# Sliding-window attention in front of two MLPs on one core: scores as plain float32 products in place of three split passes

## The chip, the cores and the metric

The kernel runs on one core of one Trainium2 chip. The metric is device time in microseconds of one execution; lower is better. Before the change three executions took 939.21, 941.5 and 942.63 us (median 941.5). The profiled execution took 941.04 us.

## What is computed

Three blocks in a row, all in float32. Attention has 4 batches, 8 heads, 576 positions and head size 64, with a causal window of 128 positions and a linear bias by distance. A gated MLP (512 to 1536) and a second MLP (512 to 2048) follow, over 2304 tokens. The reference, cut to what matters:

```python
scores = scale * np.matmul(q, k.transpose(0, 1, 3, 2))      # scale = 1/8
scores = np.where((rel >= 0) & (rel < 128), scores + bias, -1e9)
attn = softmax(scores)
x = np.matmul(attn, v)                                      # to 2304 x 512
g = x @ w_gate; x = (silu(g) * (x @ w_val)) @ w_out         # 512 -> 1536 -> 512
g = x @ w_in;   return silu(g) @ w_out2                     # 512 -> 2048 -> 512
```

## The kernel before, in words

Tokens are taken in 18 tiles of 128. Tiles 0 to 5 are part 0, 6 to 11 part 1, 12 to 17 part 2; the MLPs run part by part on 768 tokens. Each tile has two halves (`hf`) of four heads, so there are 36 halves.

The MLP products want nearly float32 accuracy. Their operands are split in two: a high part rounded to `float32r` and a low part that is the rest. Each product is three passes, high by high, high by low and low by high (`passes`, lines 803 to 807; `out1`, 963 to 965; `out2`, 993 to 995). Splitting costs a copy and a subtraction on the side engines for every operand. The scores use the same form:

- `prepare` (lines 389 to 425) turns k and q of one half with the identity on TensorE (`k_turn`, line 401; `q_turn`, line 409). From PSUM it writes the high part of k (`copy_op`, line 304 on ScalarE or 305 on VectorE) and of q (`q_hi`, line 412, ScalarE, with the factor -1/8). Then VectorE subtracts to get the low parts (`k_lo`, line 404; `q_lo`, line 415).
- `score` (lines 429 to 457) makes the products. For each half there are two head pairs `p`, three passes `(x, y)` and two heads `e` of a pair. The two heads lie in rows 0 to 63 and 64 to 127 of the array and write two different banks. That is 12 products of 128 weight columns by 256 moving columns (current and previous tile of keys). In tiles 0 and 9, the first of their part of the sequence, there are 128 moving columns.
- `attend` masks on VectorE (line 476, a `copy_predicated` that reads the scores), adds the bias and takes the row minimum (483), exponentiates on ScalarE (489), normalizes on GpSimd (509) and turns the weights with TensorE (526). `weigh` multiplies by v (line 563). v and the turned weights are plain float32 there, and two heads write PSUM partitions 0 to 63 and 64 to 127.

The order on each engine is not written by hand. `Plan.add` records every operation with an engine, an estimated cost in ns, a due time, the keys it reads and writes, and the PSUM bank it takes or gives back. `Plan.issue` then plays a list schedule with those costs and issues each engine's instructions in the order it found. At run time each engine keeps that order and waits on semaphores. Part 0's attention has due times over the first 45 us or so (`ramp`) and the MLP begins beside it. The attention of parts 1 and 2 is spread between MLP products. A wrong cost moves the order, not the time an instruction takes. The cost of the scores stands in line 456:

```python
plan.add("pe", 6 * 118 * len(halves) + 290, due, products, reads, list(take), take=take)
```

Of the kernel before, what the change touches and what calls it, by code (L numbers as in the profile page):

```python
# [9 lines left out]
F32 = mybir.dt.float32  # L10
F32R = mybir.dt.float32r
# [5 lines left out]
AF = mybir.ActivationFunctionType  # L17
ALU = mybir.AluOpType
PSUM = bass.MemoryType.PSUM

P = 128
# [180 lines left out]
def attention_moe_moe2_kernel(  # L202
# [34 lines left out]
    nc = tc.nc  # L237
    B, H, S, D = q.shape
# [13 lines left out]
    big = ctx.enter_context(tc.tile_pool(name="big", bufs=1))  # L252
# [3 lines left out]
    def ring(n, shape, dtype, name):  # L256
        return [big.tile(shape, dtype, name=f"{name}{i}") for i in range(n)]
# [2 lines left out]
    XOP = big.tile([P, 7, 2, 2, N], F32R, name="XOP")  # L260
    XST = big.tile([P, PT, KC, P], F32, name="XST")
    ACC = big.tile([P, PT, KC, P], F32, name="ACC")
    KR = big.tile([P, 2, H // 2, 2, P], F32R, name="KR")
    ident = big.tile([P, P], F32, name="ident")
    alibi = big.tile([P, H, P], BF16, name="alibi")
    bigt = big.tile([P, 2, P], F32, name="bigt")
# [11 lines left out]
    KLD_R = ring(2, [P, H, D], F32, "kld")  # L278
    QLD_R = ring(2, [P, H, D], F32, "qld")
    VLD_R = ring(3, [P, H, D], F32, "vld")  # L280
    QT_R = ring(2, [P, 2, 2, P], F32R, "qt")
    C_R = ring(2, [P, 4, P], F32, "c")
    ST_R = ring(2, [P, 3, 4], F32, "st")
    U_R = ring(3, [P, 4, P], F32, "u")
# [12 lines left out]
    plan = Plan(BANKS, {"mm": 6, "att": 6, "T": 1, "S": 4, "C": 2, "O": 1, "B": 4})  # L297

    def cost(kind, n):
        a, b = COST[kind]  # L300
        return a + b * n

    def copy_op(n, due, out, src, reads, writes, give=None, psum=True):
        act = lambda: nc.scalar.activation(out(), src(), AF.Copy)  # L304
        dve = lambda: nc.vector.tensor_copy(out(), src())
        plan.add(
            "act", cost("act_ps" if psum else "act", n), due, act, reads, writes, give=give,
            other=[("dve", cost("dve", n), dve, not psum, 500.0)],
        )
# [46 lines left out]
    def first(i):  # L356
        return (i * P) % S == 0
# [27 lines left out]
    def loaded(i, nm, hf):  # L385
        slot = i % (3 if nm == "v" else 2)
        return [(nm, slot, hf, r) for r in range(2)]

    def prepare(i, hf, due):
        kn, qn = KLD_R[i % 2], QLD_R[i % 2]  # L390
        kr = KR[:, :, 2 * hf:2 * hf + 2, i % 2, :]
        bk, bq = Bank("T"), Bank("T")
        pk = lambda: bk.tile.rearrange("p (a b) -> p a b", b=P)
        pq = lambda: bq.tile.rearrange("p (a b) -> p a b", b=P)
        slot = (2 * i + hf) % len(QT_R)
        qt = QT_R[slot]

        def k_turn():
            for j in range(2):
                h = 4 * hf + 2 * j  # L400
                nc.tensor.transpose(pk()[:, j, :], kn[:, h:h + 2].rearrange("p h d -> p (h d)"), ident)

        def k_lo():
            nc.vector.tensor_tensor(kr[:, 1], pk()[:, 0:2], kr[:, 0].bitcast(F32), ALU.subtract)

        def q_turn():
            for j in range(2):
                h = 4 * hf + 2 * j
                nc.tensor.transpose(pq()[:, j, :], qn[:, h:h + 2].rearrange("p h d -> p (h d)"), ident)

        def q_hi():
            nc.scalar.activation(qt[:, 0], pq()[:, 0:2], AF.Copy, scale=-0.125)

        def q_lo():
            nc.vector.scalar_tensor_tensor(
                qt[:, 1], pq()[:, 0:2], -0.125, qt[:, 0].bitcast(F32), ALU.mult, ALU.subtract
            )

        kk, qk = ("KR", i % 2, hf), ("qt", slot)
        plan.add("pe", 2 * 109, due, k_turn, loaded(i, "k", hf) + ["ident"], [bk], take=bk)  # L420
        copy_op(256, due, lambda: kr[:, 0], lambda: pk()[:, 0:2], [bk], [kk])
        plan.add("dve", cost("dve", 256), due, k_lo, [bk, kk], [kk], give=bk)
        plan.add("pe", 2 * 109, due, q_turn, loaded(i, "q", hf) + ["ident"], [bq], take=bq)
        plan.add("act", cost("act_ps", 256), due, q_hi, [bq], [qk])
        plan.add("dve", cost("dve", 256), due, q_lo, [bq], [qk], give=bq)

    def score(i, halves, due):

        s = i % 2
        banks = {hf: (Bank("S"), Bank("S")) for hf in halves}

        def products():
            for hf in halves:
                qt = QT_R[(2 * i + hf) % len(QT_R)]  # L440
                for p in range(2):
                    for x, y in ((0, 0), (0, 1), (1, 0)):
                        for e in range(2):
                            rows = slice(64 * e, 64 * e + 64)
                            view = banks[hf][e].tile.rearrange("p (a b c) -> p a b c", a=2, b=2)
                            rhs, dst = KR[rows, y, 2 * hf + p], view[:, p]
                            if first(i):
                                rhs, dst = rhs[:, s], dst[:, 0]
                            nc.tensor.matmul(  # L449
                                dst, qt[rows, x, p, :], rhs, start=(x == 0 and y == 0), stop=(x == 1)  # L450
                            )

        reads = [("qt", (2 * i + hf) % len(QT_R)) for hf in halves]
        reads += [("KR", t, hf) for t in ((s,) if first(i) else (s, 1 - s)) for hf in halves]
        take = tuple(b for hf in halves for b in banks[hf])
        plan.add("pe", 6 * 118 * len(halves) + 290, due, products, reads, list(take), take=take)
        return banks

    def attend(i, hf, dues, banks):
# [563 lines left out]
    def attention_part(part, at):  # L1023
        for i in range(part * PT, part * PT + PT):
            load(i, "k", at(i) - 14820.0)
            load(i, "q", at(i) - 20070.0)
            load(i, "v", at(i) - 7670.0)
            for halves in [(0,), (1,)] if i < EARLY else [(0, 1)]:
                t0 = at(i + 0.5 * halves[0])
                for hf in halves:  # L1030
                    prepare(i, hf, t0 - 8000.0)
                banks = score(i, halves, t0)
                for hf in halves:
                    attend(i, hf, [at(i + p / NP) for p in (2 * hf, 2 * hf + 1)], banks[hf])
                weigh(i, halves, at(i + 0.5 * halves[-1] + 1 / NP))
# [136 lines left out]
```

## Time and profile before

| What | Value |
|---|---|
| profiled execution | 941.04 us, span 939.3 us |
| median of three runs | 941.5 us |
| TensorE matmul (PE) busy | 916.3 us, 98% |
| VectorE (DVE) busy | 669.3 us, 71% |
| ScalarE (ACT) busy | 503.4 us, 54% |
| GpSimd (POOL) busy | 352.3 us, 38% |

Busy time of PE includes the time in which a matmul drains, so 98% is not 98% of its peak. A line number names the line of the kernel that issued an instruction; 304, 305, 313 and 314 are lines of helpers (a copy on ScalarE or VectorE, a sum on VectorE or GpSimd). PEld is TensorE's weight load, which overlaps PE. One product in the program can show as one or two matmul records in the trace.

### The profile page before, as it was taken

How to read it: one execution, taken by the hardware profiler on the slowest of the kernel's cores; microseconds unless marked ns; L12 is line 12 of the kernel's file. 1: busy time of each engine (PE TensorE's matmuls, PEld its weight loads, DVE VectorE, ACT ScalarE, POOL GpSimd, SP SyncE). 2: the span in 40 equal slices, each digit the busy share in tenths (PEclk: the TensorE clock that was granted, in tenths of full speed). 3: DMA queues.
4: the chain of work that ended last, by engine and by line, in shares of the span. 5: the costliest groups of instructions: out<-in, count | busy, mean ns of one | idle time of the engine just before them, and what ended most of it. 6: DMA issues, size and time to landing. Idle time of an engine off the chain costs nothing.

```text
span 939.3 us, 16799 instructions
## 1 busy us (share of the span) xinstructions
PE 916.3 (98%) x5626; PEld 845.3 (90%) x5626; DVE 669.3 (71%) x1536; ACT 503.4 (54%) x1276; POOL 352.3 (38%) x416
## 2 busy tenths in 40 slices
PE   7999999998999999999999999999999999999998
PEld 5799899998888888999999888888899999988887
DVE  8988779879889888637574847567735555855655
ACT  6887567757867675654343564354343322553331
POOL 3865568776657578772122512111100000300000
PEclk9999999999999999999999999999999999999999
DMA  9987997895897987986666655445576666655422
GB/s 226 280 250 244 289 316 242 275 334 176 278 304 261 301 297 266 335 294 204 189 201 188 174 186 162 169 153 172 187 238 211 205 212 210 201 185 179 157 91 90
DMA packets 156855, 209.79 MB, mean 223 GB/s; under 512 B 65760, under 2 KB 86496, under 8 KB 156768
## 3 DMA queue, kind: packets, MB, share of 16 engines
q1 hardware_dynamic: 156768, 208.71, 69.3%
q8 instruction: 45, 0.74, 0.3%
q14 instruction: 42, 0.34, 0.1%
HBM read 149.42 MB, written 59.24 MB: 222 GB/s over the span
## 4 chain that ended last, share of the span: by engine, by line
PE 76%; DVE 10%; DMA 5%; ACT 4%; POOL 3%; issue 3%; SPq 0%; DVEq 0%; POOLq 0%; ACTq 0%
PE bank L805 13%; PE bank L806 12%; PE bank L807 12%; PE bank L993 6%; PE bank L995 6%; PE bank L994 6%; PE bank L963 4%; PE bank L965 4%; PE bank L964 4%; PE bank L563 3%; PE bank L449 3%; DVE word L707 2%; PE bank L526 1%; DMA raw<-in_moe_w_out_dram 1%; DMA raw<-in_moe_w_in_dram 1%
## 5 line engine op out<-in xcount | busy, mean ns | idle before, releaser
L805 PE MATMUL bank<-XOP,wu 128*128 128x384 f32 (+1 forms) x868 | 297.2, 342 | 8.4 <-ACT tmp L304 2.6
L806 PE MATMUL bank<-XOP,wu 128*128 128x384 f32 (+1 forms) x868 | 289.6, 334 | 3.7 <-POOL XOP L314 3.0
L807 PE MATMUL bank<-XOP,wu 128*128 128x384 f32 (+1 forms) x868 | 289.4, 333 | 0.0
L805 PEld LDWEIGHTS bank<-XOP,wu 128*128 128x128 f32 x868 | 163.6, 188 | 17.8 <-ACT tmp L304 5.2
L806 PEld LDWEIGHTS bank<-XOP,wu 128*128 128x128 f32 x868 | 163.8, 189 | 6.0 <-POOL XOP L314 3.5
L807 PEld LDWEIGHTS bank<-XOP,wu 128*128 128x128 f32 x868 | 163.6, 189 | 0.2
L304 ACT ACTIVATE tmp<-bank 128x384 f32<-128x384 f32 x156 | 73.2, 489 | 108.6 <-PE bank L807 71.8
L314 POOL TENSOR_TENSOR h<-tmp,h 128x384 fp32r<-128x384 f32 x48 | 51.4, 1079 | 187.0 <-ACT h L304 185.7
L993 PE MATMUL bank<-wo,h 128*128 128x512 f32 x290 | 115.8, 399 | 0.3 <-DVE bank L649 0.3
L995 PE MATMUL bank<-wo,h 128*128 128x512 f32 x290 | 114.0, 393 | 0.0
L994 PE MATMUL bank<-wo,h 128*128 128x512 f32 x290 | 113.9, 393 | 0.0
L1005 DVE TENSOR_TENSOR ACC<-bank,ACC 128x512 f32<-128x512 f32 (+1 forms) x127 | 85.3, 681 | 26.9 <-PE bank L995 26.7
L845 DVE TENSOR_TENSOR bank<-bank,tmp 128x384 f32<-128x384 f32 x108 | 60.5, 561 | 57.8 <-PE bank L807 43.4
L963 PE MATMUL bank<-h,wo 128*128 128x384 f32 (+1 forms) x296 | 99.3, 335 | 0.1
L965 PE MATMUL bank<-h,wo 128*128 128x384 f32 (+1 forms) x296 | 98.3, 332 | 0.0
L964 PE MATMUL bank<-h,wo 128*128 128x384 f32 (+1 forms) x296 | 98.0, 331 | 0.0
L977 DVE TENSOR_TENSOR ACC<-bank,ACC 128x384 f32<-128x384 f32 x120 | 65.5, 553 | 28.1 <-PE bank L965 27.8
L922 DVE SCALAR_TENSOR_TENSOR tmp<-tmp,bank 128x384 f32<-128x384 f32 (+1 forms) x101 | 53.9, 542 | 44.3 <-ACT tmp L912 31.4
L304 ACT ACTIVATE h<-tmp 128x384 fp32r<-128x384 f32 x81 | 42.0, 522 | 70.6 <-PE bank L994 45.7
L912 ACT ACTIVATE tmp<-bank 128x384 f32<-128x384 f32 (+1 forms) x131 | 62.1, 483 | 32.0 <-PE bank L807 18.1
L509 POOL TENSOR_TENSOR c<-c,st 128x512 f32<-128x512 f32 x36 | 39.6, 1101 | 98.4 <-DVE st L506 83.2
L489 ACT ACTIVATE c<-c,st 128x128 f32<-128x128 f32 x144 | 56.3, 394 | 25.6 <-DVE st L483 25.5
(96 smaller groups left out, 1642.5 us busy)
## 6 DMA issues: line engine op xcount, KB each, us to landing
wo<-kept_o SPq DMA_DIRECT2D x56, 512.0 KB, 4.0
wu<-kept_i SPq DMA_DIRECT2D x112, 256.0 KB, 3.3
wu<-kept_g SPq DMA_DIRECT2D x72, 256.0 KB, 3.6
wu<-kept_v SPq DMA_DIRECT2D x72, 256.0 KB, 4.0
raw<-in_moe_w_out_dram SPq DMA_DIRECT2D x28, 512.0 KB, 4.8
kept_o<-wo SPq DMA_DIRECT2D x28, 512.0 KB, 4.2
kept_i<-wu SPq DMA_DIRECT2D x56, 256.0 KB, 4.3
kept_g<-wu SPq DMA_DIRECT2D x42, 256.0 KB, 4.8
```

The source lines that it names most:

```text
L304: act = lambda: nc.scalar.activation(out(), src(), AF.Copy)
L805: nc.tensor.matmul(ps, wh, xh, start=start, stop=False, skip_group_check=True)
L806: nc.tensor.matmul(ps, wh, xl, start=False, stop=False, skip_group_check=True)
L807: nc.tensor.matmul(ps, wl, xh, start=False, stop=stop, skip_group_check=True)
L963: nc.tensor.matmul(ps[:, 0:n], wh, h[:, 0], start=(i == 0), stop=False)
L964: nc.tensor.matmul(ps[:, 0:n], wh, h[:, 1], start=False, stop=False)
L965: nc.tensor.matmul(ps[:, 0:n], wl, h[:, 0], start=False, stop=(i == 1))
L977: plan.add("dve", cost("dve", n), due, lambda: nc.vector.tensor_tensor(acc, pv(), acc, ALU.add), [b], keys, give=b)
L993: nc.tensor.matmul(ps, hh, wh, start=(i == 0), stop=False)
L994: nc.tensor.matmul(ps, hh, wl, start=False, stop=False)
L995: nc.tensor.matmul(ps, hl, wh, start=False, stop=(i == 1))
L1005: plan.add("dve", cost("dve", n), due, lambda: nc.vector.tensor_tensor(acc, pv(), acc, ALU.add), [b], keys, give=b)
```

## The change

q and k are no longer split. `KR` and the `qt` buffers lose their axis of two and become plain float32. `prepare` keeps the two turns, one copy of k and one scaled copy of q, and loses both subtractions. Each bank is given back by the copy. `score` makes one plain float32 product per head, four per half, and its planned cost becomes 2 * 236 per half.

```diff
-    KR = big.tile([P, 2, H // 2, 2, P], F32R, name="KR")
+    KR = big.tile([P, H // 2, 2, P], F32, name="KR")
-    QT_R = ring(2, [P, 2, 2, P], F32R, "qt")
+    QT_R = ring(2, [P, 2, P], F32, "qt")
...
-        def k_lo():
-            nc.vector.tensor_tensor(kr[:, 1], pk()[:, 0:2], kr[:, 0].bitcast(F32), ALU.subtract)
...
-        def q_hi():
-            nc.scalar.activation(qt[:, 0], pq()[:, 0:2], AF.Copy, scale=-0.125)
-
-        def q_lo():
-            nc.vector.scalar_tensor_tensor(
-                qt[:, 1], pq()[:, 0:2], -0.125, qt[:, 0].bitcast(F32), ALU.mult, ALU.subtract
-            )
+        def q_copy():
+            nc.scalar.activation(qt, pq()[:, 0:2], AF.Copy, scale=-0.125)
...
-        copy_op(256, due, lambda: kr[:, 0], lambda: pk()[:, 0:2], [bk], [kk])
-        plan.add("dve", cost("dve", 256), due, k_lo, [bk, kk], [kk], give=bk)
+        copy_op(256, due, lambda: kr, lambda: pk()[:, 0:2], [bk], [kk], give=bk)
...
-        plan.add("act", cost("act_ps", 256), due, q_hi, [bq], [qk])
-        plan.add("dve", cost("dve", 256), due, q_lo, [bq], [qk], give=bq)
+        plan.add("act", cost("act_ps", 256), due, q_copy, [bq], [qk], give=bq)
...
-                    for x, y in ((0, 0), (0, 1), (1, 0)):
-                        for e in range(2):
-                            rows = slice(64 * e, 64 * e + 64)
...
-                            nc.tensor.matmul(
-                                dst, qt[rows, x, p, :], rhs, start=(x == 0 and y == 0), stop=(x == 1)
-                            )
+                    for e in range(2):
+                        rows = slice(64 * e, 64 * e + 64)
...
+                        nc.tensor.matmul(dst, qt[rows, p, :], rhs, start=True, stop=True)
...
-        plan.add("pe", 6 * 118 * len(halves) + 290, due, products, reads, list(take), take=take)
+        plan.add("pe", 2 * 236 * len(halves) + 290, due, products, reads, list(take), take=take)
```

The line numbers of the changed kernel are smaller: line 449 becomes 438, 409 becomes 406, 476 becomes 463, 483 becomes 470, 526 becomes 513, 563 becomes 550, 707 becomes 694.

On PE, one half of an early tile before (names are `out<-moving,weights`; `bank` is a PSUM bank, `KR` and `qt` hold k and q, `u` and `l` the turned attention weights, `vld` is v):

```order
L449 MATMUL bank_140<-KR,qt_125 128x256
L449 MATMUL bank_138<-KR,qt_125 128x256
L449 MATMUL bank_140<-KR,qt_125 128x256
L449 MATMUL bank_138<-KR,qt_125 128x256
L449 MATMUL bank_140<-KR,qt_125 128x256
L449 MATMUL bank_138<-KR,qt_125 128x256
L449 MATMUL bank_140<-KR,qt_125 128x256
L449 MATMUL bank_138<-KR,qt_125 128x256
L449 MATMUL bank_140<-KR,qt_125 128x256
L449 MATMUL bank_138<-KR,qt_125 128x256
L449 MATMUL bank_140<-KR,qt_125 128x256
L449 MATMUL bank_138<-KR,qt_125 128x256
```

and with the change, with the products by v that stand behind it:

```order
L438 MATMUL bank_140<-KR,qt_125 128x256
L438 MATMUL bank_141<-KR,qt_125 128x256
L438 MATMUL bank_140<-KR,qt_125 128x256
L438 MATMUL bank_141<-KR,qt_125 128x256
L550 MATMUL bank_135<-u_130,vld_121 64x128 x2
L550 MATMUL bank_135<-l_134,vld_122 64x128 x2
L550 MATMUL bank_135<-u_130,vld_121 64x128 x2
L550 MATMUL bank_135<-l_134,vld_122 64x128 x2
```

Twelve products of a half have become four; in all, PE's list shrinks from 5036 to 4748 rows, by 288 = 36 x 8.

On DVE, the first instructions behind the constants, before (`m_up` and `bigt` are masks and fill values, `c` and `st` scores and their row sums):

```order
L415 SCALAR_TENSOR_TENSOR qt_124<-bank_135,qt_124 128x256
L415 SCALAR_TENSOR_TENSOR qt_125<-bank_136,qt_125 128x256
L404 TENSOR_TENSOR KR<-bank_137,KR 128x2x128
L404 TENSOR_TENSOR KR<-bank_138,KR 128x2x128
L476 COPY_PREDICATED bank_139<-m_up,bigt 128x2x128
L483 ISA c_126,st_128<-bank_139,alibi 128x128
```

and with the change, the same place and, apart, the first copy of k that VectorE takes from ScalarE:

```order
L463 COPY_PREDICATED bank_139<-m_up,bigt 128x2x128
L470 ISA c_126,st_128<-bank_139,alibi 128x128
...
L492 TENSOR_SCALAR st_128<-st_128 128x4
L493 RECIPROCAL st_128<-st_128 128x4
L305 COPY KR<-bank_138 128x2x128
L492 TENSOR_SCALAR st_129<-st_129 128x4
```

The four subtractions ahead of the first mask are gone. Over the program VectorE loses 36 of each kind and takes 3 of the 36 copies of k; ScalarE keeps the other 33.

## Rows read from the trace of the kernel before

**Rows 1.** The page, busy time, share and instructions of each engine.
```profile
PE 916.3 (98%) x5626; PEld 845.3 (90%) x5626; DVE 669.3 (71%) x1536; ACT 503.4 (54%) x1276; POOL 352.3 (38%) x416
```
**Rows 2.** Busy time by stretch: stretch, length, engines' busy us (instructions), granted clock, DMA.
```profile
0.00:46.00 46.00, 38.57 (x335) 30.41 (x336) 39.05 (x166) 34.76 (x119) 25.30 (x34) 1.00 0.97 256
...
60.00:400.00 340.00, 330.37 (x2079) 304.09 (x2079) 286.78 (x635) 236.50 (x606) 231.86 (x276) 0.99 0.85 279
400.00:660.00 260.00, 258.73 (x1607) 239.86 (x1607) 163.28 (x386) 119.36 (x303) 70.38 (x81) 1.00 0.60 188
660.00:939.00 279.00, 274.69 (x1482) 258.43 (x1478) 168.57 (x312) 100.98 (x212) 15.62 (x15) 1.00 0.55 182
```
**Rows 3.** The chain of waits, first 50 us: start, length, what.
```profile
22.55 0.33 DVE KR L404
...
23.87 0.34 DVE KR L404
...
27.36 0.89 PE bank L449 x12
...
41.04 0.33 DVE KR L404
...
42.82 0.32 DVE qt L415
...
45.45 0.42 DVE KR L404
```
**Rows 4.** Groups of instructions on DVE, whole run: count, busy us, mean ns.
```profile
L404 DVE TENSOR_TENSOR KR<-bank,KR 128x256 fp32r<-128x256 f32 x36 | 15.0, 417 | 7.3 <-ACT KR L304 7.1
L415 DVE SCALAR_TENSOR_TENSOR qt<-bank,qt 128x256 fp32r<-128x256 f32 x36 | 14.9, 415 | 3.5 <-ACT qt L412 3.4
```
**Rows 5.** The same groups, 0 to 46 us.
```profile
L404 DVE TENSOR_TENSOR KR<-bank,KR 128x256 fp32r<-128x256 f32 x11 | 4.5, 412 | 1.1 <-ACT KR L304 1.1
L415 DVE SCALAR_TENSOR_TENSOR qt<-bank,qt 128x256 fp32r<-128x256 f32 x10 | 4.0, 411 | 0.6 <-ACT qt L412 0.5
```
**Rows 6.** Timeline of PE, score products: start, busy us, line, records.
```profile
135.10 1.65 PE L449 MATMUL bank<-KR,qt 64*128 64x256 f32 x24
136.68 0.45 PE L805 MATMUL bank<-XOP,wu 128*128 128x384 f32 x1
```
```profile
241.84 1.56 PE L449 MATMUL bank<-KR,qt 64*128 64x128 f32 x24
243.33 0.50 PE L993 MATMUL bank<-wo,h 128*128 128x512 f32 x1
```
**Rows 7.** The same, 323.6 to 324.3 us; and line 449's records, min/median/max ns.
```profile
323.39 1.09 PE L449 MATMUL bank<-KR,qt 64*128 64x256 f32 x16
```
```profile
L449 PE MATMUL bank<-KR,qt x432: 270/273/579, 6.3 to 623.4; 64*128 64x256 f32 x128, 64*128 64x128 f32 x16
```
**Rows 8.** Timeline of PE, products by v in plain float32.
```profile
115.36 0.39 PE L563 MATMUL bank<-u,vld 128*64 128x128 f32 x4
...
116.45 0.39 PE L563 MATMUL bank<-l,vld 128*64 128x128 f32 x4
```
**Rows 9.** Line 449 by stretch: PE and PEld busy us (records).
```profile
46.00:660.00 614.00, 22.62 (x324) 19.70 (x324) 1.00 0.74 240
```
**Rows 10.** Timeline of PE, score products near the start.
```profile
8.41 1.55 PE L449 MATMUL bank<-KR,qt 64*128 64x128 f32 x12
...
11.05 1.90 PE L449 MATMUL bank<-KR,qt 64*128 64x256 f32 x12
```
**Rows 11.** Who waited for whom on PE, 60 to 400 us: total us, times, longest.
```profile
PE bank L805 <- DVE tmp L860: 2.4, 3, 1.1
...
PE bank L805 <- DVE tmp L305: 1.7, 2, 1.0
```
**Rows 12.** The same on DVE, whole run.
```profile
DVE bank L476 <- PE bank L449: 5.2, 8, 1.6
```

More of the change, by code (lines that the diff above doesn't have):

```diff
@@ L390, in prepare @@
         kn, qn = KLD_R[i % 2], QLD_R[i % 2]
-        kr = KR[:, :, 2 * hf:2 * hf + 2, i % 2, :]
+        kr = KR[:, 2 * hf:2 * hf + 2, i % 2, :]
         bk, bq = Bank("T"), Bank("T")
@@ L441, in products @@
                 for p in range(2):
-                    for x, y in ((0, 0), (0, 1), (1, 0)):
-                        for e in range(2):
-                            rows = slice(64 * e, 64 * e + 64)
[L445 to L448, printed above, removed]
-                            nc.tensor.matmul(
-                                dst, qt[rows, x, p, :], rhs, start=(x == 0 and y == 0), stop=(x == 1)
-                            )
+                    for e in range(2):
+                        rows = slice(64 * e, 64 * e + 64)
+                        view = banks[hf][e].tile.rearrange("p (a b c) -> p a b c", a=2, b=2)
+                        rhs, dst = KR[rows, 2 * hf + p], view[:, p]
+                        if first(i):
+                            rhs, dst = rhs[:, s], dst[:, 0]
+                        nc.tensor.matmul(dst, qt[rows, p, :], rhs, start=True, stop=True)
         reads = [("qt", (2 * i + hf) % len(QT_R)) for hf in halves]
```

## The prediction

> **What bounds the kernel now.** I read the page's busy time first: PE is busy 98% of the span, DVE 71% [rows 1]. Then I split the span by stretch. From 60 us on PE is busy 330 of 340, 259 of 260 and 275 of 279 us [rows 2]. There, TensorE time added or removed is span added or removed. The first 46 us are different: PE is busy 38.6 us and DVE 39.1 [rows 2], and the chain of waits runs through DVE and ACT as well as PE. Five pieces of that chain are the subtractions that the change deletes [rows 3]. So the change has two separate accounts: PE time after 46 us, and the start.
>
> **VectorE: removed work.** 36 subtractions for k and 36 for q, 15.0 + 14.9 = 29.9 us [rows 4]. Nothing is added but three copies of k from ScalarE, which I price like a subtraction of the same size, 0.42 us each [rows 4].
>
> - *Start.* The pieces on the chain are 0.33 + 0.34 + 0.33 + 0.32 + 0.42 = 1.74 us [rows 3]. Two groups of score products also lie on it, the one at 27.36 us [rows 3] and another like it at 32 us; each grows by 0.17 (below). Net -1.74 + 0.34 = -1.4 us. Bounds: 0, if a chain right behind takes over (ACT has 34.8 us of work in these 46 [rows 2]); and 4.5 + 4.0 = 8.5 us if DVE alone sets the pace [rows 5]. I take -1.4, because the chain changes engine too often for DVE to be the only limit.
> - *After 46 us.* DVE is not the limit, so its work there is worth only the waits it causes. PE waits 2.4 + 1.7 = 4.1 us for two DVE lines between 60 and 400 us [rows 11]. In the whole run the removed work is 4.5% of DVE's busy time (29.9 of 669 [rows 1, 4]), so I cost it at nothing; PE's own dense work covers it. Bounds 0 and -4.1.
>
> **TensorE: products.** Before: 24 records for a tile, two at a time (one per head, in different rows of the array). The tile takes 136.68 - 135.10 = 1.58 us [rows 6], 0.79 per half. The pace inside is (1.09 - 0.273)/7 = 0.117 us per pair of records [rows 7]; 6 x 0.117 = 0.70, which leaves 0.09 per half for entry and exit.
>
> After: four float32 products per half. No row shows a float32 product with 64 rows and 256 moving columns. The nearest is the product by v: float32 on both sides, two heads side by side, 128 moving columns [rows 8]. Those rows come in fours, and a four is what the program issues as two products: each float32 product is two records. From 115.36 to 116.45 are five fours, 1.09/5 = 0.218 us per four, or 0.109 per pair of records with 128 columns. With 256 columns I take twice that, 0.218. A half then has 2 head pairs x 2 records = 4 pairs of records: 4 x 0.218 + 0.09 = 0.96 us, +0.17 against 0.79.
>
> After 46 us there are 324/12 = 27 halves [rows 9]. Two belong to tile 9 with 128 columns: now (243.33 - 241.84)/2 = 0.745 each [rows 6], then 4 x 0.109 + 0.09 = 0.53, -0.22. Sum: 25 x 0.17 - 2 x 0.22 = **+3.8 us**, all on the path, for PE is full there. Bounds. Below: a record of 256 columns keeps today's 0.117, a half takes 4 x 0.117 + 0.09 = 0.56, and the sum is -25 x 0.23 - 2 x 0.22 = -6.2. Above: the two heads do not run side by side, 8 x 0.218 + 0.09 = 1.83, and the sum is 25 x 1.04 + 2 x 0.22 = +26.4. I take +3.8, by the row that shares the data type.
>
> The Trainium skill (FP8 and Floating Point Precision, TensorE Precision Notes) says that true float32 takes four passes through the array. Against three passes now, at today's 0.117 a pass, it would make a half 8 x 0.117 + 0.09 = 1.03 us and the sum +5.6 in place of +3.8. The trace agrees in kind (two records, 0.109 for 128 columns); no run here shows it for these products yet.
>
> In the first 17 us TensorE runs at half the pace: 12 records of 128 columns take 1.55 us at 8.41 [rows 10], as long as 24 do later [rows 6], although the granted clock of the stretch reads 1.00 [rows 2]. Two halves with 128 columns drop from 12 to 8 records (-0.5 each). Two with 256 go from 12 records to 8 of double length (+0.5 each, on 1.90 with a wait in it [rows 10]). They cancel.
>
> **What costs nothing.** The turns on TensorE, the copies on ScalarE and all DMAs stay. Smaller `KR` and `qt` free memory nobody asked for. Banks of the turns return one subtraction earlier; that is part of the start.
>
> **Sum.** 941.04 - 1.4 + 3.8 = 943.4 us against the profiled execution, which is 0.5 below the median of the runs. A measurement of this kernel can tell about 0.5% (4.7 us) from no change, so this is **no change**.
>
> **Rivals.**
> - *A: a float32 record costs what a split record costs.* For it: score products with 128 columns take 1.49 us a tile, nearly the 1.58 of those with 256 [rows 6]. Something other than columns holds a pair of records near 0.11, and the 0.109 of the products by v [rows 8] may be that floor, not a slower rate. Against: nothing else in the rows. Time: -6.2, and the start with two groups 0.23 shorter, -2.2: 941.04 - 8.4 = 932.6. Faster. Chance 0.13. The Trainium skill (TensorE: Matmul & The Clock Gate, Back-to-back issue gap) points this way: columns/2.4 + 2.5 ns, with no word on the data type, 109 ns for 256 columns.
> - *B: the heads no longer overlap in float32.* Time 943.4 + 26.4 - 3.8 = 966. Against: the products by v do overlap, though by output columns rather than by rows [rows 8]. Chance 0.07.
> - *C: VectorE set the start alone.* -8.5 + 0.3 in place of -1.4: 936.6, and down to 932.5 if the 4.1 us of waits go too. Faster. For it: DVE is the busiest engine of the first 46 us, 39.1 against 38.6 and 34.8 [rows 2]. Chance 0.14.
> - *D: the plan is wrong by more than before.* It books 472 ns per half for products that take 4 x 0.218 = 0.87, where today it books 708 for 0.70. Each group ends 0.40 us per half later than the order assumes. The masks of line 476 stand early in DVE's queue, so they block the sums behind them that free banks for the MLP. DVE already waits 5.2 us there [rows 12]. It decides once DVE has no slack left to absorb 0.4 us, likeliest between 60 and 400 us (287 of 340 busy). If the 0.40 reaches PE in full: 27 x (0.40 - 0.17) = +6.2, 949.6 us. Slower. Chance 0.14.
>
> The change does what it says: PE's list is 288 products shorter.
>
> **How the numbers follow.** Forecast 0.52, A 0.13, C 0.14, D 0.14, B 0.07: faster 0.26 (A and most of C), same 0.52, slower 0.22 (D and B, and 0.01 of drift in the order). The range reaches from A to D, 932 to 950, and leaves out B and the far end of the bounds.
>
> **What would show it.** Line 438: 288 records, pairs 0.218 us apart, a tile in about 1.9 us. Line 404 and 415 gone from DVE, whose busy time falls to about 640 us. The first MLP products dense some 1 to 2 us earlier. A pair at 0.117 means A; 16 records one after the other means B; the dense part beginning 5 us or more earlier means C; DVE's wait for line 438 above 12 us in total, with PE waiting for lines 964 or 992, means D. The forecast is wrong if line 438 is not slower per half, or if the first 46 us shrink by more than 4.

## The result, and the profile after

The change is slower. Its median of five executions is 950.23 us (948.68 to 953.54) against 941.5 (939.21 to 943.86), ratio 1.0097 with a 95% interval of 1.0069 to 1.0125, some 9 us. The forecast was 943.4 and no change, with a range of 932 to 950. The profiled execution took 951.49 us, span 949.5.

First the products. The timeline of PE in the changed kernel shows a tile with 256 moving columns, and tile 9 with 128 (start, busy us, line, records). They answer to [rows 6]:

```profile
168.31 2.00 PE L438 MATMUL bank<-KR,qt 64*128 64x256 f32 x16
170.24 0.44 PE L792 MATMUL bank<-XOP,wu 128*128 128x384 f32 x1
```
```profile
249.16 1.16 PE L438 MATMUL bank<-KR,qt 64*128 64x128 f32 x16
250.25 0.50 PE L980 MATMUL bank<-wo,h 128*128 128x512 f32 x1
```

A tile now takes 170.24 - 168.31 = 1.93 us, where the split one took 1.58; the forecast was 1.92. Tile 9 takes 1.09, forecast 1.06, before 1.49. The part of the same tile up to 169.9 us counts 14 records and ends 0.22 earlier:

```profile
168.31 1.78 PE L438 MATMUL bank<-KR,qt 64*128 64x256 f32 x14
```

So one more pair of records is 0.22 us, twice the 0.109 that 128 columns take [rows 8].

VectorE lost the 72 subtractions, but its busy time fell from 669.3 to 649.0 us only; the forecast was about 640. The page's busy line after, beside [rows 1]:

```profile
PE 921.1 (97%) x5482; PEld 845.5 (89%) x5482; DVE 649.0 (68%) x1483; ACT 501.9 (53%) x1272; POOL 338.2 (36%) x401
```

It has 53 instructions fewer, not 72: three are the copies of k, and 16 more came over because the planner chooses the engine too (GpSimd has 15 fewer, ScalarE 4 fewer with those copies). In the kernel `old_order` below exactly the 72 are gone, and VectorE's busy time is 647.4. A subtraction whose record lasts 0.42 us [rows 4] therefore frees only 21.9/72 = 0.30 us of busy time: neighbouring records overlap.

Neither account explains 9 us. The busy time by stretch, after and, below it, before, shows where they are (stretch, length, then busy us and instructions of PE, PEld, DVE, ACT, POOL, then the granted clock):

```profile
0.00:100.00 100.00, 85.73 (x675) 72.74 (x676) 73.89 (x271) 69.65 (x230) 52.45 (x67) 0.95 0.84 236
100.00:400.00 300.00, 292.53 (x1724) 265.10 (x1724) 245.27 (x524) 207.39 (x522) 199.63 (x238) 1.00 0.85 283
400.00:660.00 260.00, 257.95 (x1547) 240.44 (x1546) 153.58 (x365) 120.31 (x303) 68.24 (x79) 0.99 0.59 190
```
```profile
0.00:100.00 100.00, 92.50 (x784) 81.21 (x785) 87.53 (x306) 74.82 (x240) 57.30 (x73) 1.00 0.90 254
100.00:400.00 300.00, 290.37 (x1763) 265.80 (x1762) 249.97 (x533) 208.20 (x523) 208.96 (x248) 0.99 0.85 282
```

In the first 100 us TensorE idles 14.3 us after the change and 7.5 before, and its mean clock there is 0.95 in place of 1.00. From 100 to 400 us it idles less than before, 7.5 against 9.6. Every engine is busy for less of the first 100 us, though of the engines beside TensorE only VectorE lost work. TensorE comes late to the MLP: its first MLP product starts at 28.43 us, before at 25.53 (the forecast was dense products 1 to 2 us earlier):

```profile
28.43 0.36 PE L792 MATMUL bank<-XOP,wu 128*128 128x256 f32 x1
```
```profile
25.53 0.39 PE L805 MATMUL bank<-XOP,wu 128*128 128x256 f32 x1
```

PE's longest waits of that stretch, after and before (who waited for whom: total us, times, longest), but for one of 3.3 us for the constants that both have:

```profile
PE bank L438 <- ACT c L476: 2.2, 1, 2.2
PE bank L550 <- DVE h L313: 1.9, 1, 1.9
PE bank L438 <- ACT KR L304: 1.4, 1, 1.4
PE bank L793 <- DVE XOP L578: 1.3, 1, 1.3
```
```profile
PE bank L526 <- POOL c L509: 1.8, 2, 1.2
PE bank L409 <- DVE KR L404: 1.2, 1, 1.2
```

Two places can be seen in the timeline. The first is on ScalarE near 11 us:

```profile
10.48 0.39 ACT L476 ACTIVATE c<-c,st 128x128 f32<-128x128 f32 x1
10.77 0.19 ACT L476 ACTIVATION_READ_ACCUMULATOR c<-c,st 128x1 f32 x1
10.87 0.36 ACT L409 ACTIVATE qt<-bank 128x256 f32<-128x256 f32 x1
11.13 0.36 ACT L304 ACTIVATE KR<-bank 128x256 f32<-128x256 f32 x1
```

TensorE had turned k of tile 1 at 9.08 us; the copy that the scores read (line 304) starts at 11.13, behind the exponentials of tile 0 and a copy of q that the new order put ahead of it. The scores start at 11.88. The view puts their wait of 2.2 us down to the next exponential on ScalarE (line 476), which they do not read; `early_copies` below shows that the copy's place is what matters. The second place is at 85 us, on PE and DVE:

```profile
84.17 1.53 DVE L694 SCALAR_TENSOR_TENSOR word<-raw,top 128x512 int32<-128x512 int32 x1
...
85.18 0.34 PE L794 MATMUL bank<-XOP,wu 128*128 128x384 f32 x1
85.62 0.55 DVE L909 SCALAR_TENSOR_TENSOR bank<-tmp,bank 128x384 f32<-128x384 f32 x1
...
87.43 0.65 PE L550 MATMUL bank<-u,vld 128*64 128x128 f32 x4 [1.91 <-DVE h L313]
...
90.67 0.41 PE L794 MATMUL bank<-XOP,wu 128*128 128x256 f32 x1
...
90.88 0.41 PE L792 MATMUL bank<-XOP,wu 128*128 128x256 f32 x1
```

VectorE works on the word of a weight for 1.53 us, with the end of a hidden layer queued behind it. TensorE waits for that, and comes back at half the clock (the level of 1.2 GHz): 256-column records start 0.21 us apart (90.67, 90.88), where 0.117 is the pace of split products of that width at full clock [rows 7]. The granted clock from 85 to 93 us is 0.66:

```profile
85.00:93.00 8.00, 5.62 (x32) 4.75 (x32) 3.96 (x7) 3.93 (x9) 3.56 (x5) 0.66 0.56 157
```

From 80 to 100 us the mean is 0.83, which is 3.4 of the 5 us by which the first 100 fall short of full clock. The rest is read from 12 to 16 us, where the kernel before runs at half pace too, although its clock reads 1.00 (twelve score records take 1.65 us at 14.47, where 24 take 1.58 later [rows 6]).

Two theories stand. ORDER: the products cost what the forecast said, and the rest is the order of instructions (and their share among the engines) that the planner found for the changed list. PRODUCTS: the longer groups hold up what waits for them and so cost all of it.

### The profile page after: what moved, and what is told of

Read it like the earlier page. It is cut to its first block, busy times and chain, and to the rows that moved or that the text cites. A ratio compares the mean times of both kernels' runs of the same rounds, so it can differ in the third digit from the quotient of the medians.

```text
span 949.5 us, 16431 instructions
## 1 busy us (share of the span) xinstructions
PE 921.1 (97%) x5482; PEld 845.5 (89%) x5482; DVE 649.0 (68%) x1483; ACT 501.9 (53%) x1272; POOL 338.2 (36%) x401
## 4 chain that ended last, share of the span: by engine, by line
PE 73%; DVE 11%; DMA 7%; ACT 4%; POOL 3%; issue 2%; SPq 1%; POOLq 0%; DVEq 0%; ACTq 0%
PE bank L792 13%; PE bank L793 12%; PE bank L794 12%; PE bank L980 5%; PE bank L982 5%; PE bank L981 5%; PE bank L950 4%; PE bank L952 4%; PE bank L951 4%; PE bank L438 3%; DMA raw<-in_moe_w_in_dram 3%; PE bank L550 3%; DMA raw<-in_moe_w_out_dram 2%; DVE word L694 2%; DVE bank L636 2%
## 5 line engine op out<-in xcount | busy, mean ns | idle before, releaser
L314 POOL TENSOR_TENSOR h<-tmp,h 128x384 fp32r<-128x384 f32 x42 | 44.1, 1057 | 172.0 <-ACT h L304 168.8
```

## The experiments

### Taking the change apart

Each ratio below is against executions of the kernel before taken beside that run (medians 940.01, 940.53 and 939.89 us), not against the 941.5 from which the expected times were worked out. So the ratios are what to compare.

Three kernels separate products, subtractions and order. `products_alone` has the order of before on every engine; only the products change:

```diff
-    KR = big.tile([P, 2, H // 2, 2, P], F32R, name="KR")
+    KR = big.tile([P, 2, H // 2, 2, P], F32, name="KR")     # qt likewise
...
-                    for x, y in ((0, 0), (0, 1), (1, 0)):
-                        ...
+                    nc.tensor.matmul(dst, qt[rows, 0, p, :], KR[rows, 0, 2 * hf + p], start=True, stop=True)
```

> The kernel before with its order kept (planned costs and all subtractions as before), only the products are plain float32 on unsplit q and k; the low parts are still made and not read. Theory ORDER (the change costs 3.8 us of TensorE time, and the other 5 us come from the new order of instructions): 941.5 + 3.8 = 945.3 us, between 944 and 947. Theory PRODUCTS (longer groups of products hold up what waits behind them, so the products cost all of it): 950 us, between 948.5 and 952.

Measured: 945.99 us, ratio 1.0069 (1.0043 to 1.0094). About 6.5 us, between 4.0 and 8.8. ORDER's range is 0.27 to 0.58% above 941.5, PRODUCTS' 0.74 to 1.12%: the ratio lies between them, and this run alone does not decide. The products cost more than the 3.8 us of their own TensorE time.

`old_order` issues the subtractions as nothing, but still plans them:

```diff
         def k_lo():
-            nc.vector.tensor_tensor(kr[:, 1], pk()[:, 0:2], kr[:, 0], ALU.subtract)
+            pass                                            # q_lo likewise
```

> As products_alone, and the 72 subtractions of VectorE are issued as nothing: order of before, work of the change. ORDER: at or below products_alone; by the first sum 1.4 us below it, 943.9, between 941 and 946. PRODUCTS: 948 to 951, near the change. A theory that VectorE's relief is worth nothing: equal to products_alone within 1 us.

Measured: 941.8 us, ratio 1.0030 (1.0011 to 1.0049). This kernel does the change's operations in the order, and on the engines, of before, and is 0.3% slower than before, not 1.0%. PRODUCTS, 0.69 to 1.01%, falls. Against products_alone the subtractions are worth 0.39%, 3.7 us, with intervals that overlap a little.

`new_order_split_time` keeps the change's order and gives TensorE back its old time:

```diff
-                        nc.tensor.matmul(dst, qt[rows, p, :], rhs, start=True, stop=True)
+                        for x in range(3): nc.tensor.matmul(..., start=(x == 0), stop=(x == 2))
```

> The change with its order kept, but each head's product is three float32r passes over the rounded q and k (high by high, three times), so TensorE takes the time of before and the low parts are left out of the computation. ORDER: 950.2 - 3.8 = 946.4 us, between 945 and 948.5. PRODUCTS: the time of before, 940 to 942.5.

Measured: 946.31 us, ratio 1.0080 (1.0057 to 1.0104). ORDER expected 0.37 to 0.74%, PRODUCTS at most 0.1%: PRODUCTS falls again, and the ratio lies a little above ORDER's range, which its interval overlaps. With products of the old length the new order is still 0.8% slower than before. Its first 100 us look like the change's, 14.0 us of idle TensorE:

```profile
0.00:100.00 100.00, 86.01 (x740) 75.33 (x741) 74.40 (x273) 71.16 (x232) 52.98 (x68) 0.98 0.84 239
```

### Where the order loses

Two hybrids plan one part of the tiles as before (subtractions planned and issued as nothing, old cost) and the other part as the change does. The condition is all that differs:

```diff
+        kept = i < PT        # start_old_rest_new; start_new_rest_old: i >= PT
+        if kept:
             plan.add("dve", cost("dve", 256), due, k_lo, [bk, kk], [kk], give=bk)
```

> The change, where tiles 0 to 5 are planned as before (old cost of the products, the subtractions planned and issued as nothing), tiles 6 to 17 as in the change. Theory START (the new order loses its time in the first 100 us): near old_order, 0.2 to 0.5% above before, about 942 us, and no wait of 2 us for a copy of k near 9 us. Theory REST (it loses it later): near the change, 948 to 951.

Measured: 942.16 us, ratio 1.0031 (1.0016 to 1.0046).

> The other way round: tiles 0 to 5 as in the change, tiles 6 to 17 planned as before with the subtractions issued as nothing. START: near the change, 0.8 to 1.1% above before, 948 to 951 us, with the 2 us wait near 9 us. REST: near old_order, 941 to 943.

Measured: 949.82 us, ratio 1.0103 (1.0081 to 1.0125). START holds on both sides: within these intervals, the part of the order that belongs to tiles 0 to 5 makes the whole difference between the change and old_order. The stretch again, first with the old start, then with the new:

```profile
0.00:100.00 100.00, 93.18 (x734) 79.60 (x735) 80.47 (x280) 75.62 (x243) 59.06 (x72) 1.00 0.94 265
```
```profile
0.00:100.00 100.00, 88.00 (x702) 75.60 (x703) 75.33 (x277) 71.61 (x234) 52.73 (x69) 0.97 0.83 235
```

TensorE idles 6.8 us with the old start and 12.0 with the new one, and its first MLP product starts at 24.19 and at 28.01 us. The scores' waits (line 449 here) are in the second kernel too, and in no form in the first:

```profile
PE bank L449 <- ACT c L488: 2.6, 1, 2.6
PE bank L449 <- ACT KR L304: 1.4, 1, 1.4
```

### Whether one wait or one number is to blame

`early_copies` moves the copies ahead of the exponentials by their due time:

```diff
-        copy_op(256, due, lambda: kr, ...)
+        copy_op(256, due - 4000.0, lambda: kr, ...)
```

(and the copy of q likewise).

> The change with one thing more: the copies of k and q out of PSUM (one on ScalarE or VectorE, one on ScalarE) are due 4 us earlier in the plan, so that on ScalarE the copy of k for tile 1 stands ahead of the exponentials of tile 0 and not behind four of them. Theory COPY (the 2.2 us wait of TensorE near 9.5 us is the seed of the lost start): the wait is gone, dense work begins 2 us or more earlier, 945 to 947 us (0.5 to 0.7% above before). Theory SPREAD (the start is lost in many small places by an order that fits the waits badly): the wait is gone and the time stays within 0.2% of the change, 0.8 to 1.2% above before.

Measured: 947.61 us, ratio 1.0094 (1.0072 to 1.0116), where the change had 1.0097. The first MLP product starts at 25.67 us. The wait of 2.2 us is gone. In its place stand many short ones; these are the longest but for the constants:

```profile
PE bank L550 <- ACT u L304: 1.5, 2, 0.8
PE bank L438 <- ACT KR L304: 1.1, 2, 0.7
PE bank L950 <- DVE st L470: 0.8, 1, 0.8
PE bank L792 <- DVE h L313: 0.7, 1, 0.7
```

Its first 100 us have 10.7 us of idle TensorE, better than the change's 14.3, but the ratio did not follow. SPREAD holds; COPY, 0.5 to 0.7%, falls by little, for the interval begins at 0.72%, and a gain of some 0.3% over the change would still fit the two intervals.

`cost_real` books the products at what they take, `cost_old` at the number of before:

```diff
-        plan.add("pe", 2 * 236 * len(halves) + 290, ...
+        plan.add("pe", 4 * 218 * len(halves) + 90, ...     # cost_real
+        plan.add("pe", 6 * 118 * len(halves) + 290, ...    # cost_old
```

> The change with the planned cost of the products set to what the trace shows, 4 x 218 ns per half and 90 for entry and exit, in place of 2 x 236 per half and 290. If the wrong cost in the plan is what makes the new order bad: 945 us or less, with a dense start and no wait of 2 us on TensorE near 85 us. If any change of order moves the time by several us either way: anywhere from 940 to 955, with the long waits of TensorE at other places than in the change.

Measured: 949.43 us, ratio 1.0108 (1.0078 to 1.0138). A right cost does not help. Nor does it take the stall at 85 us to lose the time: in this kernel and in start_new_rest_old, as slow as the change, TensorE is busy without a break from 80 to 100 us, at full clock. These profiled executions took 946.66 and 948.26 us, that of before 941.04 (cost_real, then start_new_rest_old):

```profile
80.00:100.00 20.00, 20.00 (x144) 19.66 (x143) 18.10 (x40) 13.40 (x36) 11.12 (x14) 1.00 0.70 229
```
```profile
80.00:100.00 20.00, 20.00 (x151) 19.65 (x150) 17.40 (x45) 15.30 (x45) 12.39 (x15) 1.00 0.61 204
```

The clock takes part of the loss in another way. Over all its executions start_new_rest_old has a mean granted clock of 0.995, start_old_rest_new of 0.998. An estimate from these two: 0.003 of 945 us, some 3 of the 7.7 us between them, if TensorE is busy wherever the clock is low.

> The change with the products still booked at 6 x 118 ns per half: only the subtractions have left the plan. If the booked cost makes the bad start: 0.2 to 0.4% above before, near old_order. If the missing subtractions make it: 0.8 to 1.1% above before, near the change. If any new order loses some of it: 0.5% or more.

Measured: 946.38 us, ratio 1.0081 (1.0058 to 1.0104). It is not near old_order, so the booked cost alone is not what makes the start bad. The work itself costs 0.30% (old_order), so with the cost of before, taking the subtractions out of the plan is enough for an order that loses the other 0.5%. Whether that is due to the subtractions or to any new order, the ranges do not tell apart.

Is any other order as bad? Two kernels change nothing but the booked cost in the kernel before, to the numbers of the change and of cost_real:

> The kernel before, whole, with one number of the plan changed: the products are booked at 2 x 236 ns per half in place of 6 x 118, as the change books them. Nothing is removed or added, only the order moves. Theory TUNED (the order before is a lucky or tuned one, any shift of the plan's costs loses several us): 0.3 to 1.0% slower than before, 943 to 950 us. Theory REMOVED (the order is bad because the subtractions left the plan): within 0.3% of before.

Measured: 945.06 us, ratio 1.0054 (1.0033 to 1.0074).

> The kernel before with the products booked at 4 x 218 ns per half and 90 in place of 6 x 118 and 290: a second shift of the plan, in the other direction, nothing else. TUNED (any shift of the plan loses): 0.3 to 1.0% above before. If only booking too little loses (before_cost_a): within 0.25% of before.

Measured: 942.66 us, ratio 1.0033 (1.0016 to 1.0049). The same work in two other orders costs 0.5% and 0.3%. The first is what TUNED expected; the second lies at the lower edge of TUNED and its interval takes in the other theory's 0.25%, so it decides nothing. In the first, TensorE idles 12.2 us of the first 100:

```profile
0.00:100.00 100.00, 87.81 (x747) 75.59 (x748) 85.30 (x302) 72.36 (x232) 52.12 (x67) 1.00 0.85 236
```

In the second it idles 7.2 us there, no more than before, so what it loses is not lost in the start.

No plan that changed tiles 0 to 5 found an order as good as that of before: the change, new_order_split_time, start_new_rest_old, cost_real, cost_old, early_copies, before_cost_a and, by the least and later than the start, before_cost_b. A new order of tiles 6 to 17 alone (start_old_rest_new, 1.0031) costs no more than the work (old_order, 1.0030). Why the old start fits best is not known from the runs.

### A version of both

`mixed` takes the order of before, plain products for tiles 0 to 5, where TensorE has room, and split ones after:

```diff
+        plain = i < PT
+        k_to = KRF[...] if plain else kr[:, 0]
-                    for x, y in ((0, 0), (0, 1), (1, 0)):
+                    for x, y in ((0, 0),) if i < PT else ((0, 0), (0, 1), (1, 0)):
```

> Order of before. Tiles 0 to 5 take plain float32 products and no subtractions (but for k of tile 5, which tile 6 needs split, so it is copied twice), tiles 6 to 17 the split products of before. TensorE's extra time after 46 us is then 3 halves x 0.17 = 0.5 us. If VectorE's relief is worth its 3.7 us (old_order against products_alone) mainly at the start: 0.2 to 0.4% below before, 936 to 938 us. If it is worth it later: within 0.2% of before.

Measured: 940.5 us, ratio 1.0001 (0.9986 to 1.0016). The gain of 0.2 to 0.4% is not there. `mixed_fixed` differs in where the plain copies lie: in `mixed` they overwrote rows that the first MLP reads.

> As mixed, with the plain copies of k and q at a place that nothing else writes in that time (mixed let them overwrite rows that the first MLP reads; its time counts, its output was another one). Within 0.2% of before, 939 to 942, if VectorE's relief at the start is worth no more than the 0.5 us of longer products; 0.2% or more below, if mixed was held up by its extra waits.

Measured: 940.34 us, ratio 1.0006 (0.9991 to 1.0021). It matches before and beats it by nothing. Twenty-two subtractions fewer in tiles 0 to 5 (twelve of q, ten of k) bring no gain that can be measured; one of 0.1% would lie at the edge of the interval.

## Why the prediction was wrong, point by point

- **What bounds the kernel:** right from 100 us on, where TensorE idles 14.1 us in all against 15.5 before. The start was read as a place where removed work saves a little. It is a place where the order decides, and no row was asked about that.
- **TensorE, +3.8 us:** the price per half is right: 0.96 us was forecast, 1.93/2 = 0.965 measured. Rivals A (0.117 per pair) and B (no overlap) fall. That this is worth 3.8 us of the whole is not shown: products_alone measured 6.5, between 4.0 and 8.8. The Trainium skill (FP8 and Floating Point Precision, TensorE Precision Notes) has four passes for true float32. The trace agrees: a pair of products of 256 columns takes two records' time, 2 x 0.22 = 0.44 us, near four times the 0.117 of a float32r pass [rows 7]. The formula of the Trainium skill (TensorE: Matmul & The Clock Gate, Back-to-back issue gap) names no data type; the 109 ns worked out from it for 256 columns, an estimate, is not what plain float32 takes here, 0.22 us a record.
- **VectorE at the start, -1.4 us:** not settled. 3.7 us by products_alone against old_order, but the intervals touch, and mixed_fixed shows nothing from tiles 0 to 5. Rival C, -8.5, falls: without the subtractions old_order is slower than before, not faster. The 29.9 us of removed work added up records that overlap others; 21.9 us of busy time went (old_order).
- **The sum, +2.4 us or 0.26% for the order as it was:** right in total. old_order, which is that sum as a kernel, measured 0.30% (0.11 to 0.49). That is luck in part: as measured, the two terms are +6.5 and -3.7 us, both larger than forecast, and the excess cancels.
- **The step that failed:** "What costs nothing", and the sum built on it. The forecast counted the instructions that go and left the rest where they stand. It gave a new order no term in the sum and, as "drift in the order", a chance of 0.01. But the planner makes the whole order anew. Against old_order the change's order costs 0.97 - 0.30 = 0.67%, about 6.3 us. The hybrids, taken beside each other, differ by 949.82 - 942.16 = 7.7 us and place it in the plan of tiles 0 to 5.
- **Rival D** came nearest in time, 949.6 us, by a mechanism that did not occur. It blamed the booked cost; cost_real corrects that and stays at 1.0108. A wrong cost can make a worse start (before_cost_a, 0.54%), but by the order that it leads to. Its 0.40 us per half leaves out the 290 ns that the same line books once per call: a tile is booked at 1.23 us and took 1.93, 0.35 per half. Rival D put the loss between 60 and 400 us; TensorE idles 9.9 us there after the change (first line below) and 9.6 before [rows 2]. DVE's wait for the products did rise, from 5.2 us [rows 12] to 10.1, below the 12 that was named:

```profile
60.00:400.00 340.00, 330.14 (x2002) 299.20 (x1999) 276.33 (x614) 233.91 (x603) 221.37 (x264) 0.99 0.84 277
```
```profile
DVE bank L463 <- PE bank L438: 10.1, 12, 2.3
```

- **"The change does what it says":** it does. Lines 404 and 415 are gone and 288 records stand at line 438.

What stays open: which rows of the start's order carry the loss. One of them, the late copy of k, was taken away and the ratio stayed; another, the stall at 85 us, is missing in two kernels that are as slow. How much of the 6 us is clock is only estimated above. Why the longer products cost 6.5 us by themselves, and not 3.8, is open too.

## What to carry to other kernels

Where a list scheduler with modelled costs sets the order, an edit has two prices: its own work, and the new order. Measure them apart: keep the removed operations in the plan and issue them as nothing, and the old order stays while the work goes. The second price was in no row of the kernel before; it should widen the range. Here every other plan of the start came out slower, so the slow side was the one to widen; that this holds for other kernels is not shown.

## What the runs showed of the hardware

Plain float32 products go by columns where split ones do not. Tile 9, with half the moving columns, took 1.09 us against 1.93 in plain float32, and 1.49 against 1.58 in three float32r passes [rows 6]. So at 128 columns one plain product (two records of 0.109) is cheaper than three float32r passes, and at 256 it is dearer.

A record's length is not what the engine gains when the instruction goes. Records of neighbours overlap: on VectorE the word that starts at 84.17 us lasts 1.53 us, to 85.70, and the next instruction starts at 85.62. The 72 subtractions of 0.42 us took 21.9 us of busy time with them, 0.30 us each.
